# Delta rule into two MoE layers: another order of the first two chunks, group 0 inverted on two engines, fewer weights loaded at the start

## The chip, the cores and the metric

The kernel runs on one core of a Trainium2 chip. Its engines are TensorE (PE, with PEld for its weight loads), VectorE (DVE), ScalarE (ACT), GpSimd (POOL) and SyncE (SP), which issues every transfer. The metric is the time on the device in microseconds (us) of one execution, as a median over runs.

## The reference

Three stages in a row; each feeds the next:

```python
k_n = k / (norm(k) + 1e-6)                       # 4 batches x 8 heads, 768 steps, head size 48
for t in range(S):                               # attention by the delta rule, state D x D per head
    y[t] = q[t] @ state
    state += beta[t] * outer(k_n[t], v[t] - k_n[t] @ state)
x = y as 3072 tokens x 384
h = x @ w_in;  g = h if h >= 1, 0 if h <= -1, else (h + 1)**2 / 4;  x = g @ w_out     # 384 -> 2048 -> 384
h = x @ w_in2; g = relu(h)**2;                                      out = g @ w_out2  # the same sizes
```

## The kernel before

**Tiling.** The 768 steps are cut into 24 chunks of 32 steps; a chunk holds 128 tokens (4 batches). Chunks are gathered twice: in blocks of 2 or 3 (`SIZES`), whose tokens go through the MoE layer together, and in groups of 2 or 4 (`GROUPS`), whose triangular 32 x 32 systems are inverted together. Block 0 is chunks 0 and 1, and so is group 0; group 1 is chunks 2 to 5, group 2 chunks 6 to 9.

**A chunk.** `gram` (L268) multiplies keys with keys and queries on PE and masks the result. `tri` (L334) inverts a group's systems by forward substitution: `step(j)` (L396) is one product and one sum of j x (w-1-j) elements, w the width; a product and a sum depend on each other, so an inverse is a chain of small operations on one engine. All groups share one tile, `tx`, for the inverse; `row2` (L383) writes its start, `end` (L414) transposes the result into `gp`. Group 0 is inverted in two halves of 16 columns, both in one instruction on DVE, and put together by `joined` (L424) with matmuls `ld` and `dld`; `rows` transposes what these need into `d`. The other groups are inverted whole, on POOL. `chunk_steps` (L457) is what follows: `ks`, `tr`, `qs`, `ku`, `pu`, `xt`; the last gives the MoE's input, `xh` and its low part `xl`. `value` (L254) scales a chunk's values on POOL.

**A weight.** Weights come as 64-bit numbers: 32 tiles of 128 x 384 for layer 1 (16 of `w_in`, 16 of `w_out`, in the order in which the MoE asks for them; here x = 0 to 31). A weight's way has four steps: ACT scales it (L164), DVE joins its bits (L172, L175), ACT rounds it to the high part (L186), DVE subtracts that for the low part (L190). PE's hidden tile f (`hidden`, L565) needs both parts of weight x = 2f-1 (for f over 1), the output tile f (`out1`, L603, two hidden tiles later) those of x = 2f+2. Layer 2's weights are read back later and split on POOL and DVE (L237).

**What sets the order.** Up to L725 the kernel stands in one `manual_schedule` for all engines: every engine takes its instructions as the code is written. From L727 only PE's order is the code's. The others' is set by the framework when the kernel is built, by priorities in the code and by when its own model thinks that inputs are ready; each engine then keeps that order strictly. `more_w1` (L674) advances the conversion of layer 1's weights by one step for several weights at a time; before block 0 it runs 12 times, then once in each of the 32 slots of block 0 (two slots for each hidden tile). `put(n, slot, f)` places other work in slots: `end` of group 1 in slot 18, `tri_put` the inverses of groups 2 and on.

**The loads.** `first1(EAGER)` issues the first 18 weights on SP at the start, behind the first keys and queries; each conversion's second step lets `ahead` issue loads up to `AHEAD` = 8 further. Every raw weight has a tile of its own, whose place its two parts take over. Six of the last weights' tiles serve the first chunks before that (`spare`, L313).

Of the kernel before, what the change touches and what calls it, by code (L numbers as in the profile page):

```python
# [25 lines left out]
def kernel(  # L26
# [38 lines left out]
    EAGER = 18  # L65
    AHEAD = 8
# [129 lines left out]
    def weight_items(w):  # L196
# [137 lines left out]
    def tri(n, eng, halves=False):  # L334
# [9 lines left out]
        def two(t, rows, cols):  # L344

            a = t[:, rows, cols]
            (ps_, p_), (rs_, r_), (cs_, c_) = a.ap
            return bass.AP(a.tensor, a.offset, [[ps_, p_], [T2 * (T + 1), 2], [rs_, r_], [cs_, c_]])

# [22 lines left out]

        def row():
            if halves:
                d = two(gm, both, both)
                eng.tensor_mul(
                    d, d, r.rearrange("p (a o i) -> p a o i", a=2, o=1)
                    .to_broadcast([P, 2, T2, T2]))
                return
            for e, rs, cs in whole:  # L380
                e.tensor_mul(gm[:, rs, cs], gm[:, rs, cs], across(r, rs, cs))

        def row2():  # L383
            if halves:
                eng.tensor_mul(
                    two(x, both, both), two(gm, both, both),
                    g.rearrange("p (a i o) -> p a i o", a=2, o=1).to_broadcast([P, 2, T2, T2]))
            else:
                for e, rs, cs in whole:
                    e.tensor_mul(x[:, rs, cs], gm[:, rs, cs], down(g, rs, cs))  # L390
# [516 lines left out]
```

## Time and profile before

| | |
|---|---|
| median of 3 runs | 1054.86 us (1054.44 to 1056.35) |
| the profiled execution's own time | 1054.6 us |
| its span in the profile | 1052.9 us |
| PE busy | 989.3 us (94%), x14440 |
| DVE, ACT, POOL busy | 611.5, 454.3, 313.2 us |
| PE's busy share in the first four 40ths of the span (26.3 us each) | 0.4, 0.3, 0.5, 0.8 |
| the chain that ended last, by engine | PE 81%, DVE 11%, nothing the profile shows ("issue") 4%, ACT 2% |

PE is the engine with the most work, and from the fifth 40th on it is busy 90% or more of nearly every slice. So the time goes where PE waits: 1052.9 less 989.3 us, most of it in the first 140 us. In the rows below an operation is named by engine, line, what it writes and reads, and its size as partitions x elements; "x2" is a count; in brackets stand the engine's idle time before and what ended it. "issue" is a wait for nothing that the profile shows. A row of a stretch gives the busy time of PE, PEld, DVE, ACT and POOL in this order; PEclk is the granted clock of TensorE, 1.00 being the higher of its two levels (2.4 GHz).

### The profile page before, as it was taken

To read this page: it belongs to the slowest core of one execution; us is meant where nothing else is said; L and a number is where in the kernel's file an instruction comes from. 1 tells how busy PE (TensorE), PEld (TensorE's weight loads), DVE (VectorE), ACT (ScalarE), POOL (GpSimd) and SP (SyncE) were. 2 spreads that over 40 slices of the span, in tenths; PEclk is the share of its full clock that TensorE was granted. 3 is DMA by queue.
4 is the path that set the end of the run, shared out by engine and by line. 5 is a ranking of instruction groups with operands and counts; after the bars stand their busy time and mean duration, and the time that the engine had idled before them with its cause. 6 is when DMAs were issued, how large, how long until landed. Compare 5 with 4: busy or idle time off the path is not lost.

```text
span 1052.9 us, 33012 instructions
## 1 busy us (share of the span) xinstructions
PE 989.3 (94%) x14440; PEld 945.0 (90%) x14440; DVE 611.5 (58%) x1125; ACT 454.3 (43%) x931; POOL 313.2 (30%) x456
## 2 busy tenths in 40 slices
PE   4358898999999999999999999999999999999998
PEld 4347788898899998999999999999999999999998
DVE  6879765675575666767545577543434343444333
ACT  2346544445444444545445554433333333333332
POOL 4690681294039208608600123110101010010000
PEclk9997999999999999999999999999999999999999
DMA  9942144352451441512111223010101010000000
GB/s 297 326 121 77 33 124 134 88 150 73 130 152 48 148 134 33 167 56 70 31 42 55 77 90 121 16 45 1 45 1 46 1 45 1 24 1 24 1 23 23
DMA packets 36049, 80.89 MB, mean 77 GB/s; under 512 B 4544, under 2 KB 18368, under 8 KB 35904
## 3 DMA queue, kind: packets, MB, share of 16 engines
q1 hardware_dynamic: 35904, 78.78, 24.8%
q8 instruction: 113, 1.85, 0.8%
q14 instruction: 32, 0.26, 0.1%
HBM read 63.03 MB, written 15.73 MB: 75 GB/s over the span
## 4 chain that ended last, share of the span: by engine, by line
PE 81%; DVE 11%; issue 4%; ACT 2%; DMA 1%; SPq 0%; DVEq 0%; ACTq 0%
PE acc L555 36%; PE h L555 35%; PE tr L486 2%; PE yy L506 2%; PE sps L517 2%; PE yy L472 2%; DVE g L582 1%; DVE g L584 1%; PE g L281 1%; PE ks L472 1%; DVE gl L593 1%; DVE wl L172 1%; DVE wl L175 1%; DVE gp L415 1%; PE xt L540 1%
## 5 line engine op out<-in xcount | busy, mean ns | idle before, releaser
L555 PE MATMUL h<-xh,w 128*128 128x384 f32 (+1 forms) x1632 | 320.4, 332 | 1.8 <-ACT r L581 1.3
L555 PEld LDWEIGHTS h<-xh,w 128*128 128x128 f32 x1632 | 272.7, 190 | 6.8 <-ACT r L581 1.8
L593 DVE TENSOR_TENSOR gl<-g,gh 128x384 fp32r<-128x384 f32 (+1 forms) x272 | 169.5, 623 | 134.3 <-ACT gh L592 128.8
L592 ACT CAST gh<-g 128x384 fp32r<-128x384 f32 (+1 forms) x272 | 135.0, 496 | 209.3 <-DVE g L584 106.0
L555 PE MATMUL h<-xl,w 128*128 128x384 f32 (+1 forms) x816 | 179.8, 329 | 1.3 <-DVE xl L543 1.3
L555 PE MATMUL acc<-gh,w 128*128 128x384 f32 (+1 forms) x864 | 168.5, 331 | 3.8 <-ACT gh L592 3.8
L587 DVE TENSOR_TENSOR g<-r 128x384 f32<-128x384 f32 x128 | 71.4, 558 | 157.4 <-ACT r L586 157.4
L555 PE MATMUL acc<-w,gh 128*128 128x384 f32 x768 | 155.6, 337 | 2.0 <-DVE e L600 2.0
L586 ACT ACTIVATE r<-h,zero 128x384 f32<-128x384 f32 x128 | 74.5, 582 | 166.1 <-PE h L555 166.1
L555 PEld LDWEIGHTS acc<-gh,w 128*128 128x128 f32 x864 | 136.9, 191 | 9.8 <-ACT gh L592 4.2
L555 PEld LDWEIGHTS h<-xl,w 128*128 128x128 f32 x816 | 141.5, 190 | 1.9 <-DVE xl L543 1.9
L555 PEld LDWEIGHTS acc<-w,gh 128*128 128x128 f32 x768 | 136.3, 188 | 2.3 <-ACT gh L592 2.3
L581 ACT ACTIVATE r<-h,one 128x384 f32<-128x384 f32 (+1 forms) x144 | 78.6, 546 | 89.4 <-PE h L555 84.9
L411 POOL TENSOR_TENSOR t<-tx,gm 128x30 f32<-128x30 f32 (+9 forms) x180 | 109.6, 609 | 19.9 <-DVE tx L390 6.4
L412 POOL TENSOR_TENSOR tx<-tx,t 128x30 f32<-128x30 f32 (+9 forms) x180 | 108.4, 602 | 13.7
L584 DVE SCALAR_TENSOR_TENSOR g<-r,g 128x384 f32<-128x384 f32 (+1 forms) x144 | 88.8, 617 | 36.6 <-ACT g L583 34.8
L582 DVE TENSOR_SCALAR g<-r 128x384 f32<-128x384 f32 (+1 forms) x144 | 63.6, 442 | 79.5 <-ACT r L581 78.9
L642 POOL CAST xh<-x2r 128x1152 fp32r<-128x1152 f32 x8 | 9.5, 1186 | 292.9 <-PE h L555 246.1
L583 ACT ACTIVATE g<-g 128x384 f32<-128x384 f32 (+1 forms) x144 | 70.6, 490 | 59.4 <-DVE g L582 58.3
L555 PE MATMUL acc<-gl,w 128*128 128x384 f32 (+1 forms) x432 | 91.5, 320 | 2.6 <-DVE gl L593 2.6
L555 PE MATMUL acc<-w,gl 128*128 128x384 f32 x384 | 88.0, 337 | 0.0
L555 PEld LDWEIGHTS acc<-gl,w 128*128 128x128 f32 x432 | 72.4, 190 | 3.3 <-DVE gl L593 3.3
(94 smaller groups left out, 835.9 us busy)
## 6 DMA issues: line engine op xcount, KB each, us to landing
raw<-in_w_dram SPq DMA_DIRECT2D x64, 384.0 KB, 6.3
kqt<-in_kq_dram SPq DMA_DIRECT2D x88, 192.0 KB, 3.8
kv<-in_kv_dram SPq DMA_DIRECT2D x24, 384.0 KB, 3.1
w2f<-wl SPq DMA_DIRECT2D x32, 192.0 KB, 3.5
w2r<-w2f SPq DMA_DIRECT2D x16, 384.0 KB, 3.0
x2r<-x SPq DMA_DIRECT2D x8, 576.0 KB, 4.4
out_dram<-e SPq DMA_DIRECT2D x24, 192.0 KB, 2.0
x<-e SPq DMA_DIRECT2D x18, 192.0 KB, 2.3
```

The source lines that it names most:

```text
L411: eng.tensor_mul(t, by.to_broadcast(shape), of.to_broadcast(shape))
L412: eng.tensor_add(rest, rest, t)
L472: per_bh(lambda b, h, p, pd: nc.tensor.matmul(o[p, h], kqt[c][pd, b // 2, h, x * T:(x + 1) * T], st[pd, b // 2, h], start=h == 0, stop=x = ...
L555: nc.tensor.matmul(o, *((r, l) if swap else (l, r)), **flags)
L581: marks[0] = nc.scalar.activation(r, h, AF.Relu, bias=one)
L582: marks[1] = nc.vector.tensor_scalar(g, r, 2.0, 0.5, ALU.min, ALU.mult)
L583: nc.scalar.activation(g, g, AF.Square)
L584: nc.vector.scalar_tensor_tensor(g, r, -1.0, g, ALU.add, ALU.max)
L586: marks[0] = nc.scalar.activation(r, h, AF.Relu, bias=zero)
L587: marks[1] = nc.vector.tensor_mul(g, r, r)
L592: nc.scalar.copy(ghi, g)
L593: nc.vector.tensor_sub(glo, g, ghi.bitcast(F32))
```

## The change

1. **Group 0's inverse** runs its two halves as separate instructions, the first on DVE, the second on POOL (`halves=(V, G)`). The masks of the grams around it go from POOL to DVE, behind the inverse.
2. **The first two chunks' chain** stands in the manual part for all engines, link by link; `rows` stands ahead of `end`. The conversions' steps stand behind the chain's links: 6 of them before block 0 instead of 12, in the last half of the chain.
3. **Loads.** Ten weights are loaded at the start instead of 18. The eleventh (x = 10) takes its tile over from `cross`, so its load waits until chunk 1 has read that; loads of later chunks' keys, queries and values are ordered behind it (`quiet`). Weights from x = 17 on go through a ring of three tiles, each loaded three ahead.
4. **The low part** of weights from x = 20 on (12 of 32) is subtracted on POOL instead of DVE.

The core of the diff:

```diff
-    EAGER = 18
-    AHEAD = 8
+    EAGER = 10
+    OWN = 17
+    ALONE = 20
...
     def load_w(x, key):
         w, f, i = key
         pool, tag, bufs = ring, "raw", RAW
-        if w == 0:
+        if w == 0 and x < OWN:
             pool, tag, bufs = wp, f"w{i}{f}", 1
         raw = raws[key] = pool.tile([P, DM, 2], I32, tag=tag, bufs=bufs, name="raw")
-        nc.sync.dma_start(raw.rearrange("p a b -> p (a b)"), (w1, w2)[w][f, i].bitcast(I32))
+        with after[0]():
+            ins = nc.sync.dma_start(
+                raw.rearrange("p a b -> p (a b)"), (w1, w2)[w][f, i].bitcast(I32)
+            )
+        if w == 0 and x == EAGER:
+            after[0] = lambda: tc.issue_after(ins.ins)
...
-            nc.vector.tensor_sub(lo, box["t"], hi.bitcast(F32))
+            (nc.vector if x < ALONE else nc.gpsimd).tensor_sub(lo, box["t"], hi.bitcast(F32))
...
-            r[1] = lambda: (s1(), ahead(x + 1 + (RAW if w else AHEAD)))
+            r[1] = lambda: (s1(), ahead(x + 1 + RAW))
...
         def ahead(end):
+            if w == 0 and turn[0] is not None:
+                end = min(end, EAGER)
...
-    spare = {
-        name: f"w{i}{NF - f}" for name, i, f in
-        (("u0", 1, 1), ("u1", 1, 2), ("cross", 0, 1), ("z", 1, 3), ("l", 0, 2), ("d", 1, 4))
-    }
+    spare = {"cross": f"w1{EAGER // 2 - 1}"}
+    for x, name in enumerate(("u0", "u1", "z", "l", "d", "t")):
+        spare[name] = f"w{x % 2}{NF - 1 - x // 2}"
...
+        parts = whole
+        if halves:
+            parts = [(e, *[slice(T2 * i, T2 * i + T2)] * 2) for i, e in enumerate(halves)]
...
         def step(j):
...
+            ts = []
+            for i, e in enumerate(halves or (eng,)):
+                lo, hi = (T2 * i, T2 * i + T2) if halves else (0, T)
+                w = hi - lo - 1 - j
+                pool, tag = (wp, spare["t"]) if i else (ring, "t0")
+                t = pool.tile([P, j, w], F32, tag=tag, bufs=1, name="t")
+                ts.append((e, lo, hi, t))
+                e.tensor_mul(
+                    t,
+                    x[:, lo:lo + j, lo + j:lo + j + 1].to_broadcast([P, j, w]),
+                    gm[:, lo + j:lo + j + 1, lo + j + 1:hi].to_broadcast([P, j, w]),
+                )
+            for e, lo, hi, t in ts:
+                rest = x[:, lo:lo + j, lo + j + 1:hi]
+                e.tensor_add(rest, rest, t)
...
+    def quiet(load, c):
+        with after[0]():
+            load(c)
...
-        begin, pre, steps, end = tri(0, V, True)
+        begin, pre, steps, end = tri(0, V, (V, G))
...
-        go([gram(c, late=2, eng=G) for c in range(GFIRST[1], GFIRST[2])])
+        masks1 = [gram(c, late=2) for c in range(GFIRST[1], GFIRST[2])]
         cross_gram(0, 1)
-        masks = [gram(c, 1, 2, late=2, eng=G) for c in range(HEADS)]
+        masks = [gram(c, 1, 2, late=2) for c in range(HEADS)]
         go(steps)
         for c in range(HEADS):
             value(c)
-        go(masks)
+
+        rows0()
         end()
-        rows0()
+        for c in range(HEADS):
+            ld0(c)
+        go(masks1)
+        for c in range(HEADS):
+            dld0(c)
+        chains = [chunk_steps(c) for c in range(HEADS)]
+        (k0, t0, q0, p0, _, x0), (k1, t1_, q1, p1, _, x1) = chains
+        go([k0, t0])
         begin, pre, steps, end1 = tri(1, G)
         begin()
-        ins = go(pre[:-2])
-        behind[0] = lambda: tc.issue_after(ins.ins)
+        go(masks)
+        k1()
+        go(pre[:-2])
+        go([q0, p0, t1_])
+        go(pre[-2:])
+        go(steps)
+        more_w1(2)
+        q1()
+        x0()
+        more_w1(2)
+        p1()
+        more_w1(1)
+        x1()
+        more_w1(1)
...
-        for m, fs in enumerate([[k0, t0], [k1], [q0, p0], [t1_], [q1], [x0], [p1], [x1]]):
-            go(fs)
-            if m < 4:
-                more_w1(3)
         behind[0] = lambda ins=marks[2]: tc.issue_after(ins.ins)
         turn[0] = None
-        load_kv(HEADS)
+        first1(EAGER + RAW)
+        quiet(load_kv, HEADS)
```

How instructions stand now, at three places. The lines' numbers are each kernel's own: L411, L412, L172, L175 and L190 of before are L401, L408, L181, L184 and L199 of after.

**DVE, behind group 0's last step.** Before: `gp` is the inverse's transpose, then `d`, then group 1's start and the first conversions (`wl` from `raw`).

```order
L412 TENSOR_TENSOR tx<-tx,t 128x2x14
L415 STREAM_TRANSPOSE gp<-tx 128x32x32
L433 STREAM_TRANSPOSE d<-tx 128x16x32
L351 STREAM_TRANSPOSE gm<-gp 128x32x32
L246 RECIPROCAL st_549<-st_547 128x32
```

After, from the same place on; `kv<-kv,ks` is chunk 1's step `ks`.

```order
L408 TENSOR_TENSOR tx<-tx,t 128x14
L429 STREAM_TRANSPOSE d<-tx 128x16x32
L411 STREAM_TRANSPOSE gp<-tx 128x32x32
L308 TENSOR_TENSOR gp<-gp,mask 128x8x2x32 x4
L446 TENSOR_TENSOR gp<-gp,w 128x8x16 x2
L355 STREAM_TRANSPOSE gm<-gp 128x32x32
L308 TENSOR_TENSOR gp<-gp,mask 128x256 x2
L478 TENSOR_TENSOR kv<-kv,ks 128x384
L257 RECIPROCAL st_746<-st_744 128x32
```

`d` went ahead of `gp`, and four masks, the two joins (L446), two more masks and chunk 1's subtraction came ahead of group 1's start; the conversions stand behind that.

**POOL, in the middle of group 2's inverse** (steps 15 to 18 of 30; step j's elements are j x (31-j)). Before:

```order
L411 TENSOR_TENSOR t<-tx,gm 128x240
L412 TENSOR_TENSOR tx<-tx,t 128x15x16
L411 TENSOR_TENSOR t<-tx,gm 128x240
L412 TENSOR_TENSOR tx<-tx,t 128x16x15
L411 TENSOR_TENSOR t<-tx,gm 128x238
L412 TENSOR_TENSOR tx<-tx,t 128x17x14
L411 TENSOR_TENSOR t<-tx,gm 128x234
L257 TENSOR_TENSOR kv<-kv,nt 128x384
```

After; `w_2105`, `w_2163`, `w_2228` and `w_2286` are the weights x = 28 to 31.

```order
L401 TENSOR_TENSOR t<-tx,gm 128x240
L408 TENSOR_TENSOR tx<-tx,t 128x15x16
L401 TENSOR_TENSOR t<-tx,gm 128x240
L199 TENSOR_TENSOR w_2105<-wl,w_2105 128x384
L408 TENSOR_TENSOR tx<-tx,t 128x16x15
L199 TENSOR_TENSOR w_2163<-wl,w_2163 128x384
L268 TENSOR_TENSOR kv<-kv,nt 128x384
L401 TENSOR_TENSOR t<-tx,gm 128x238
L199 TENSOR_TENSOR w_2228<-wl,w_2228 128x384
L408 TENSOR_TENSOR tx<-tx,t 128x17x14
L199 TENSOR_TENSOR w_2286<-wl,w_2286 128x384
```

The last four low parts stand among steps 16 and 17 of the inverse; five more (x = 23 to 27) stand among its steps 4 to 10, and three (x = 20 to 22) ahead of its first step.

**PE, at the end of block 0**, after: `h` is a hidden tile, `acc` an output tile.

```order
L502 MATMUL yy<-kv,gp 32x48 x32
L551 MATMUL h<-xh,w_2163 128x256 x6
L551 MATMUL h<-xl,w_2163 128x256 x3
L536 MATMUL xt<-ident,kv 128x128 x3
L551 MATMUL acc_1265<-gh,w_2105 128x256 x2
```

PE's order is the same in both kernels; `w_2163` is what hidden tile 15, the last of block 0, multiplies with.

## Rows read from the trace of the kernel before

**Rows 1.** Stretches: start:end, length, busy us (count) per engine, PEclk, DMA share, GB/s.

```profile
15.00:55.00 40.00, 15.78 (x758) 14.52 (x751) 35.96 (x73) 14.13 (x31) 24.64 (x35) 1.00 1.04 340
...
60.00:66.00 6.00, 4.49 (x106) 3.46 (x107) 0.90 (x2) 2.53 (x6) 5.29 (x10) 1.00 0.23 68
...
66.00:102.00 36.00, 26.57 (x461) 23.98 (x464) 35.73 (x78) 23.04 (x54) 14.29 (x23) 0.81 0.27 79
```

**Rows 2.** Chain that ended last: start us, length us, what.

```profile
27.02 2.07 DVE gp L415
...
30.76 2.31 issue
...
49.93 1.50 PE ks L466 x64
...
58.91 1.43 issue
```

**Rows 3.** Timeline (start us, us, engine, line, what, idle before): inverse of group 0.

```profile
15.19 0.18 DVE L411 TENSOR_TENSOR t<-tx,gm 128x28 f32<-128x28 f32 x1
...
19.64 2.52 POOL L297 TENSOR_TENSOR gp<-gp,mask 128x512 f32<-128x512 f32 x2 [6.41 <-ACT gp L294]
...
19.67 1.36 DVE L411 TENSOR_TENSOR t<-tx,gm 128x108 f32<-128x108 f32 x1
```

**Rows 4.** DVE by line, 66.1 to 81 us: count, busy us, mean ns.

```profile
L175 DVE SCALAR_TENSOR_TENSOR wl<-wt,wl 128x384 int32<-128x384 int32 x7 | 5.3, 771 | 0.0
...
L190 DVE TENSOR_TENSOR w<-wl,w 128x384 fp32r<-128x384 f32 x7 | 5.0, 718 | 0.0
...
L172 DVE TENSOR_SCALAR wl<-raw 128x384 int32<-128x384 uint32 x7 | 4.6, 662 | 0.0
```

**Rows 5.** The same, 81 to 102.2 us.

```profile
L175 DVE SCALAR_TENSOR_TENSOR wl<-wt,wl 128x384 int32<-128x384 int32 x12 | 6.7, 557 | 0.0
...
L190 DVE TENSOR_TENSOR w<-wl,w 128x384 fp32r<-128x384 f32 x11 | 6.3, 571 | 0.0
...
L172 DVE TENSOR_SCALAR wl<-raw 128x384 int32<-128x384 uint32 x11 | 3.9, 354 | 0.0
...
L297 DVE TENSOR_TENSOR gp<-g,mask 128x512 f32<-128x512 f32 x3 | 2.1, 684 | 0.0
```

**Rows 6.** Timeline: DVE and POOL around the first conversions.

```profile
32.21 0.35 DVE L246 RECIPROCAL st<-st 128x32 f32<-128x32 f32 x1 [0.42 <-ACT st L245]
...
34.61 2.12 DVE L172 TENSOR_SCALAR wl<-raw 128x384 int32<-128x384 uint32 x4
...
37.41 0.48 POOL L411 TENSOR_TENSOR t<-tx,gm 128x30 f32<-128x30 f32 x1 [1.43 <-DVE tx L390]
...
41.89 0.29 DVE L450 TENSOR_TENSOR gp<-gp,w 128x128 f32<-128x128 f32 x1 [2.42 <-PE w L445]
```

**Rows 7.** Timeline: DVE, POOL and PE, hidden tiles 5 to 15 of block 0.

```profile
101.82 0.42 DVE L593 TENSOR_TENSOR gl<-g,gh 128x256 fp32r<-128x256 f32 x1
...
110.24 2.13 DVE L415 STREAM_TRANSPOSE gp<-tx 128x1024 f32<-128x1024 f32 x1
...
117.16 0.22 DVE L391 COPY tx<-st 128x32 f32<-128x32 f32 x1
...
119.27 0.24 POOL L412 TENSOR_TENSOR tx<-tx,t 128x30 f32<-128x30 f32 x1
...
138.41 0.80 POOL L412 TENSOR_TENSOR tx<-tx,t 128x240 f32<-128x240 f32 x1
...
116.08 1.65 PE L555 MATMUL acc<-gh,w 128*128 128x256 f32 x6
...
135.41 0.98 PE L555 MATMUL h<-xh,w 128*128 128x256 f32 x6
```

**Rows 8.** POOL by line and shape, whole span: count, busy us, mean ns.

```profile
L237 POOL TENSOR_TENSOR w<-w2r,w 128x384 fp32r<-128x384 f32 x16 | 16.6, 1039 | 60.1 <-ACT w L231 57.6 <-PE acc L555 2.5
```

**Rows 9.** The page's DMA issues: tile, queue, op, count, KB each, us to landing.

```profile
raw<-in_w_dram SPq DMA_DIRECT2D x64, 384.0 KB, 6.3
```

More of the change, by code (lines that the diff above doesn't have):

```diff
@@ L115 @@
     kqt, kvt, gp, nt, xh, xl = {}, {}, {}, {}, {}, {}
+    marks = [None] * 3
     def load_kq(c):
@@ L148 @@
     raws = {}
+    after = [nullcontext]
     def load_w(x, key):
@@ L205, in item @@
             if w == 0:
-                r = part_stages(keys[x], box)
+                r = part_stages(x, keys[x], box)
             else:
@@ L288, in gram @@
             kqg.pop(c)
-            if late < 2:
+            if turn[0] is None:
                 load_kg(c + KG)
@@ L332, with tri @@
     T2 = T // 2
-    def tri(n, eng, halves=False):
+    def tri(n, eng, halves=()):
         x = tx
@@ L342, in flat @@
             return t.rearrange("p j i -> p (j i)")[:, diag]
[L344 to L348, printed above, removed]
         def begin():
@@ L371, in gamma2 @@
             return nc.vector.tensor_mul(g, g, bet[:, n, :])
+        parts = whole
+        if halves:
+            parts = [(e, *[slice(T2 * i, T2 * i + T2)] * 2) for i, e in enumerate(halves)]
         def row():
[L374 to L380, printed above, removed]
+            for e, rs, cs in parts:
                 e.tensor_mul(gm[:, rs, cs], gm[:, rs, cs], across(r, rs, cs))
         def row2():
[L384 to L390, printed above, removed]
+            for e, rs, cs in parts:
+                e.tensor_mul(x[:, rs, cs], gm[:, rs, cs], down(g, rs, cs))
             nc.vector.tensor_copy(flat(x), g)
@@ L396, in step @@
         def step(j):
-            if halves:
-                w = T2 - 1 - j
-                t = ring.tile([P, 2, j, w], F32, tag="t0", bufs=1, name="t")
-                rest = two(x, slice(0, j), slice(j + 1, T2))
-                by = two(x, slice(0, j), slice(j, j + 1))
-                of = two(gm, slice(j, j + 1), slice(j + 1, T2))
-                shape = [P, 2, j, w]
-            else:
-                w = T - 1 - j
-                t = ring.tile([P, j, w], F32, tag="t0", bufs=1, name="t")
-                rest = x[:, 0:j, j + 1:T]
-                by = x[:, 0:j, j:j + 1]
-                of = gm[:, j:j + 1, j + 1:T]
-                shape = [P, j, w]
-            eng.tensor_mul(t, by.to_broadcast(shape), of.to_broadcast(shape))
-            eng.tensor_add(rest, rest, t)
+            ts = []
[13 more added lines that the diff above has]
+                e.tensor_add(rest, rest, t)
         def end():
@@ L718 @@
             value(c)
-        go(masks)
+        rows0()
         end()
-        rows0()
+        for c in range(HEADS):
[6 more added lines that the diff above has]
+        go([k0, t0])
         begin, pre, steps, end1 = tri(1, G)
         begin()
-        ins = go(pre[:-2])
-        behind[0] = lambda: tc.issue_after(ins.ins)
+        go(masks)
[12 more added lines that the diff above has]
+        more_w1(1)
     ENGINES = {mybir.EngineType.PE}
     with tc.manual_schedule(engines=ENGINES):
-        for f in (ld0, dld0):
-            for c in range(HEADS):
-                f(c)
-        go(pre[-2:])
-        go(steps)
-        chains = [chunk_steps(c) for c in range(HEADS)]
-        (k0, t0, q0, p0, _, x0), (k1, t1_, q1, p1, _, x1) = chains
-        for m, fs in enumerate([[k0, t0], [k1], [q0, p0], [t1_], [q1], [x0], [p1], [x1]]):
-            go(fs)
-            if m < 4:
-                more_w1(3)
         behind[0] = lambda ins=marks[2]: tc.issue_after(ins.ins)
         turn[0] = None
-        load_kv(HEADS)
+        first1(EAGER + RAW)
+        quiet(load_kv, HEADS)
         for c in range(KG):
-            load_kg(KQ + KG + c)
+            quiet(load_kg, KQ + KG + c)
         SL = 2 * NF
```

6 lines of the change are left out of this document (2 added, 4 removed).

## The prediction

> **What bounds the kernel now.** The page's slices say that PE is busy 90% or more from about 130 us on, so the change, which touches only the first two chunks and the 32 weights of layer 1, can win or lose only before that. I read three things there, in this order.
>
> First the chain of waits up to 66 us [rows 2]. It leaves DVE with the inverse's transpose at 27.0 us and runs through PE's small matmuls; `ks`, 64 of them, takes 1.50 us. Between those PE stops five times for "issue", from 2.31 us at 30.8 to 1.43 us at 58.9, together 19.0 us. No instruction and no transfer of the program ends these stops. They fall where the transfers are saturated (DMA share 1.04, 340 GB/s from 15 to 55 us); from 60 to 66, with a share of 0.23, there is none [rows 1]. I read them as PE's own code waiting behind the weights.
>
> Second the stretch from 66 to 102 us [rows 1]: DVE is busy 35.7 of 36 us, PE 26.6 at a mean clock of 0.81. Block 0 has begun, but DVE is the bound. It converts weights, and until about 81 us at a worse price than later: the three DVE steps of one take 0.771 + 0.718 + 0.662 = 2.15 us [rows 4] beside POOL's inverse of group 1, and 0.557 + 0.571 + 0.354 = 1.48 us after it [rows 5].
>
> Third the end of block 0 [rows 7]: from about 102 us PE is the bound, and it reaches hidden tile 15 at 135.4 us. POOL meanwhile inverts group 2 and nobody waits for it. That is what the change alters most.
>
> **The front, part by part.** *Inverse of group 0.* Now one instruction of 28 elements costs DVE 0.18 us [rows 3]; the change gives DVE 28 of half the size and POOL as many. A POOL operation of 30 elements takes 0.24 us [rows 7], with the gap to the next about 0.32, so 28 take 9.0 us, with a little for sizes up to 56 about 10. If the engines hold each other up in every pair, DVE's 28 x 0.2 = 5.6 come on top: 15.7. From a start at 15.5 us (one product more on POOL ahead of it) this ends between 25.5 and 31.2 us; I take 27.5, nearer to the low end, because such small operations hold little. The old inverse ended at 27.0. So the split in itself wins nothing; what POOL's masks cost the old one (1.36 us for an operation beside a POOL mask [rows 3]) goes into it.
>
> The row first: at 19.67 us a DVE product that otherwise takes under 0.3 us took 1.36, until the POOL mask begun at 19.64, of 1.26 us apiece, was done [rows 3]. The Trainium skill says why: "SBUF — State Buffer", section "Who interferes with whom", has VectorE and GpSimd share a pair of SBUF ports by an exclusive lock, which a VectorE operation with two SBUF inputs needs. By that rule alone the two halves would go one after the other; the trace agrees for large operations, and no row shows two small ones side by side. This is the second rival.
>
> *The chain.* From 27.5: the transpose 2.07 [rows 2], four masks that are now on DVE ahead of the join, at 0.684 each for this size [rows 5], 2.7; the join 0.29 [rows 6]; `tr` and `ks` at 1.50 each [rows 2]; an evacuation and a subtraction at about 0.57 [rows 5], 1.1. That is 36.7 us for chunk 1's subtraction. `d` is transposed beside POOL's half, and `ld` with it, so they cost nothing; were that cover gone, 1.0 and 2 us. Group 1's start then takes what it took from 32.21 to 37.41 less the four conversion steps in between, 2.12 [rows 6]: 3.1 us. With 0.7 for stops that remain the conversions begin at 40.5 us, where they began at 34.6 [rows 6]: 5.9 later. The stops themselves go because ten weights are 3.9 MB, 11.6 us at 340 GB/s, so the transfers are done some 27 us into the span.
>
> *What DVE has to do by the end of hidden tile 5's work, at 102.2 us* (101.82 + 0.42 [rows 7]). In the old order 27 low parts stand ahead of that and 30 of the two steps before; in the new 20 and 23. Seven conversions fewer, at 1.48 less the overlap of neighbours, about 1.25: 8.7 us won. DVE's idle time is filled: 2.4 us [rows 6] and 6.0 - 0.9 = 5.1 us [rows 1], 7.5 us won at most, nothing at least. The later start loses 5.9. POOL's inverse of group 1 now runs beside busy DVE where 7.5 us of it were beside an idle one: 7.5 x (1 - 1.48/2.15) = 2.3 lost. Together **8.0 us earlier**; bounds 3 (idle mostly not filled, start a little late) and 9.4, since PE has no more than 36 - 26.6 = 9.4 us to give [rows 1].
>
> *Loads.* x = 10 waits on SP for chunk 1's `qs`, and the loads of x = 11 and 12, values, keys and queries are queued behind it; ten conversions lie between, over 20 us at 2.15, so I cost it at nothing. From x = 20 on a load waits for the conversion three ahead of it: 3 x 1.25 = 3.8 us against 6.3 to landing [rows 9], at worst 2.5 us in each of four turns, 10 us on ACT and DVE. There PE is the bound, and the same weights are late on POOL anyway, so this is not added.
>
> **The end of block 0.** The low parts of x = 23 to 29 stand in POOL's queue among the first 16 steps of group 2's inverse, and POOL keeps its order. That inverse can't begin before `end` of group 1, since `tx` is shared. Before, `end` starts at 110.24, the diagonal's copy is done at 117.38, POOL's step 1 at 119.51 and step 16 at 139.21 [rows 7]: nothing needed it. Now DVE's queue from `end` to that copy holds 2.13 + two times 0.354 + 0.684 + two of about 0.57 + two times 0.557 + 0.22 = 6.0 us; add the same 2.1 to the end of step 1; 19.7 to the end of step 16, as before; and seven low parts at 1.04 [rows 8], 7.3. So x = 29 is ready 35.1 us after `end` starts. Hidden tile 15, which needs it, came 135.41 - 110.24 = 25.2 us after: it will be **9.9 us late**, tile 14 a part of that (x = 27). Bounds: 4.5, if POOL does a low part in DVE's 0.571 and step 1 needn't wait; 13.9, if each also waits for one DVE operation. DVE gets 12 x 0.571 us back, but it isn't the bound there. Chunk 6, the next that needs group 2, comes much later.
>
> Behind a wait PE is slow at first: six matmuls took 1.65 us behind its wait for chunk 2, and 0.98 in the stream [rows 7]; two such sets, **1.3 us** (0.7 to 2).
>
> **Sum.** - 8.0 + 9.9 + 1.3 = + 3.2 us. Span 1052.9 to 1056.1, own time 1054.6 to 1057.8; the median lies 0.26 above the profiled run: **1058.1 us**. From the bounds the case goes from - 4.2 (9.4 won, 4.5 and 0.7 lost) to + 12.9 (3 won, 13.9 and 2 lost).
>
> **Rivals.** *The low parts are in time (faster).* If POOL reached x = 29 within 25.2 us of `end`, only the front counts: 1054.9 - 8.0 = 1046.9 us. It decides where 30 operations and 7 low parts take 25.2 - 8.1 = 17.1 us, 0.46 each; the 30 took 0.66 [rows 7]. For it: POOL is otherwise idle there, and the inverse could start earlier than I think. Against it: the order puts 16 steps ahead, and the steps' times are measured.
>
> *The two halves go one after the other.* The inverse ends at 31.2 instead of 27.5, all later work on DVE 3.7 us later: 1058.1 + 3.7 = 1061.8 us. It is the rule above as a mechanism of this kernel; the large operations speak for it, the small size of these against.
>
> *The stops stay.* If half of the 19.0 us remain though the weights are fewer, the front loses instead: 1058.1 + 9.5 = 1067.6 us. Rows 1 speak against it.
>
> **How the numbers follow.** Forecast 0.55, low parts in time 0.22, halves serial 0.17, stops stay 0.06. Within 0.2%, some 2.1 us, about what a measurement of this kernel can tell from no change: 0.17 of the forecast's 0.55, 0.02 and 0.01 of the next two, 0.20. Faster: 0.05 of the forecast and 0.20 of the first rival, 0.25. Slower: 0.33 + 0.16 + 0.06 = 0.55. The range leaves out the lower half of the first rival and the top of the last: 1047 to 1067 us.
>
> **What would show it.** In the changed kernel's trace: PE's stops before block 0 a few us in all instead of 19; POOL's half done at 25 to 31 us; the first hidden tile some 15 us earlier than now; tile 5's work done near 94 us; then PE waiting at tiles 14 and 15 for POOL's L199, some 10 us together. No such wait on POOL would prove me wrong, and so would DVE still being late at tile 5.

## The result and the profile after

The changed kernel takes 1066.49 us (median of 4 runs, 1064.07 to 1068.01) against 1054.93 us of the kernel before on the same chip: ratio 1.0105, 95% interval 1.0082 to 1.0128, so 11.6 us slower. The direction was forecast, and the time is inside the range, 0.5 us below its upper end; the loss forecast was 3.2 us. The profiled execution took 1068.0 us, its span 1066.3.

The page's busy times of PE, DVE and POOL after, and its chain by engine:

```profile
PE 994.7 (93%) x14440; PEld 949.4 (89%) x14440; DVE 616.6 (58%) x1119; ACT 452.9 (42%) x931; POOL 330.8 (31%) x492
...
PE 81%; DVE 8%; issue 4%; DMA 3%; POOL 3%; ACT 1%; SPq 1%; DVEq 0%; ACTq 0%; POOLq 0%
```

PE has the same 14440 matmuls. Of the 13.4 us by which this span is longer, 5.4 are matmuls that took longer (994.7 instead of 989.3 us, at a mean granted clock of 0.976 instead of 0.990) and 8.0 are waits. POOL, 3%, is new on the chain, and DMA has 3% instead of 1%. The stretches of [rows 1] after (start:end, length, busy us of PE, PEld, DVE, ACT, POOL, granted clock, DMA share, GB/s):

```profile
15.00:55.00 40.00, 24.16 (x1011) 22.01 (x1007) 28.35 (x67) 12.00 (x27) 18.69 (x47) 0.89 0.46 158
60.00:66.00 6.00, 1.10 (x64) 0.94 (x64) 6.00 (x9) 2.55 (x6) 5.45 (x8) 0.77 1.04 306
66.00:102.00 36.00, 21.77 (x338) 19.02 (x338) 34.25 (x60) 18.99 (x43) 27.55 (x37) 0.71 0.46 133
```

PE does 24.2 us of work in the first stretch instead of 15.8, so the chain did get ahead. From 66 to 102 us DVE is nearly as full as before, but POOL is busy 27.6 us beside it instead of 14.3, and PE does 21.8 us instead of 26.6. Where the lead goes shows in the start of block 0's hidden tiles (us, from PE's timeline; counted as in the prediction, tile 16 is block 1's first):

| hidden tile | before | after | difference |
|---|---|---|---|
| 0 | 65.68 | 52.31 | -13.4 |
| 3 | 82.83 | 73.62 | -9.2 |
| 5 | 93.09 | 90.97 | -2.1 |
| 7 | 102.55 | 101.99 | -0.6 |
| 8 | 104.78 | 108.43 | +3.6 |
| 12 | 123.05 | 126.65 | +3.6 |
| 14 | 131.23 | 142.80 | +11.6 |
| 16 | 137.93 | 151.03 | +13.1 |

After tile 16 the two run alike. So there are two losses: 12.8 us between tiles 0 and 7, nearly all of it ahead of tile 5, where DVE never rests, and 13.7 us from there to tile 16.

### The profile page after: what moved, and what is told of

Same layout as the page of the kernel before. It is cut to its first block, busy times and chain, and to the rows that moved or that the text cites. A ratio compares the mean times of both kernels' runs of the same rounds, so it can differ in the third digit from the quotient of the medians.

```text
span 1066.3 us, 33065 instructions
## 1 busy us (share of the span) xinstructions
PE 994.7 (93%) x14440; PEld 949.4 (89%) x14440; DVE 616.6 (58%) x1119; ACT 452.9 (42%) x931; POOL 330.8 (31%) x492
## 3 DMA queue, kind: packets, MB, share of 16 engines
q1 hardware_dynamic: 35904, 78.78, 24.5%
## 4 chain that ended last, share of the span: by engine, by line
PE 81%; DVE 8%; issue 4%; DMA 3%; POOL 3%; ACT 1%; SPq 1%; DVEq 0%; ACTq 0%; POOLq 0%
PE acc L551 35%; PE h L551 35%; PE g L292 2%; PE tr L482 2%; PE yy L502 2%; DMA raw<-in_w_dram 1%; PE yy L468 1%; PE sps L513 1%; DVE g L579 1%; PE ks L468 1%; DVE g L577 1%; DMA kqt<-in_kq_dram 1%; DVE gl L588 1%; POOL tx L408 1%; POOL t L401 1%
## 5 line engine op out<-in xcount | busy, mean ns | idle before, releaser
L551 PE MATMUL h<-xh,w 128*128 128x384 f32 (+1 forms) x1632 | 323.7, 335 | 7.1 <-ACT r L576 4.9
L551 PEld LDWEIGHTS h<-xh,w 128*128 128x128 f32 x1632 | 275.7, 192 | 12.5 <-ACT r L576 5.9
L408 POOL TENSOR_TENSOR tx<-tx,t 128x84 f32<-128x84 f32 (+18 forms) x194 | 114.3, 589 | 14.4
L401 POOL TENSOR_TENSOR t<-tx,gm 128x84 f32<-128x84 f32 (+18 forms) x194 | 111.8, 576 | 18.2 <-DVE tx L387 4.0
L579 DVE SCALAR_TENSOR_TENSOR g<-r,g 128x384 f32<-128x384 f32 (+1 forms) x144 | 92.1, 640 | 38.2 <-ACT g L578 36.4
L577 DVE TENSOR_SCALAR g<-r 128x384 f32<-128x384 f32 (+1 forms) x144 | 63.0, 438 | 79.0 <-ACT r L576 78.1
```

The source lines that it names most:

```text
L401: e.tensor_mul(t, x[:, lo:lo + j, lo + j:lo + j + 1].to_broadcast([P, j, w]), gm[:, lo + j:lo + j + 1, lo + j + 1:hi].to_broadcast([P, j, w]),
L408: e.tensor_add(rest, rest, t)
L551: nc.tensor.matmul(o, *((r, l) if swap else (l, r)), **flags)
L577: marks[1] = nc.vector.tensor_scalar(g, r, 2.0, 0.5, ALU.min, ALU.mult)
L579: nc.vector.scalar_tensor_tensor(g, r, -1.0, g, ALU.add, ALU.max)
```

## The experiments

The theories: **C**, DVE pays for every instruction that runs beside POOL's inverse of group 1; **L**, the later weights' loads hold ACT; **P**, POOL's low parts are late (the prediction's); **S**, PE's stops for "issue" set the chain; **F** and **O**, the conversions start too late, or stand in the wrong order. The comparisons' kernel before took 1053.8, 1054.6 and 1054.1 us (medians) beside the first, second and third group of runs, so a difference of two kernels' medians can differ by some 1 us from that of their ratios. A tile's start comes from one profiled execution: tile 0 started at 52.31 us in the changed kernel and at 53.95 in the first run below, whose instructions up to there are the same, so a difference of 1.6 us or less between two profiles shows nothing by itself.

### The end of block 0: low parts and loads

`e1_low_dve`: `- ALONE = 20`, `+ ALONE = 99`.

> The changed kernel, with all low parts left on DVE (none on POOL). Theory P (POOL's late low parts hold the conversions' buffers and hidden tiles 13 to 15): DVE's 2.67 us stop for POOL at 131.7 us, PE's 2.80 us for the subtraction behind it and the 1.26 us of tile 15 go, block 1's first hidden tile starts 5 to 9 us earlier than 151.0, and the whole takes 1058 to 1061 us against 1066.5. Theory L (the later weights' loads, three ahead, hold ACT): its 5.8 us of stops for loads stay, DVE gets 12 more subtractions of 0.56 us, and the time is 1064 to 1070 us.

1066.2 us, ratio 1.0112 (1.0082 to 1.0141): the same as the changed kernel. Tile 16 starts at 152.4. PE's wait for POOL is gone, but its waits for DVE's subtraction (3.4 us) and ACT's copy (3.0 us) stay. Theory P falls.

`e2_deep_loads`:

```
-    OWN = 17
+    OWN = 99
-            r[1] = lambda: (s1(), ahead(x + 1 + RAW))
+            r[1] = lambda: (s1(), ahead(x + 1 + (RAW if w else 8)))
-        first1(EAGER + RAW)
+        first1(EAGER + 8)
```

> The changed kernel, with the weights from the 18th on loaded into their own places too and eight ahead instead of three. Theory L: ACT's 5.8 us of stops for loads (94 to 129 us) go, tile 13 starts some 4 us earlier, and the whole takes 1060 to 1063 us. Theory P: ACT's stops go too, but POOL's low parts are as late as before, so block 1 starts within 1.5 us of 151.0 and the time is 1065 to 1068 us.

1059.8 us, ratio 1.0052 (1.0037 to 1.0067): 6.7 us faster than the changed kernel (5.6 by the two ratios). ACT waits for no load any more, tile 16 starts at 144.45 instead of 151.03. What it cured, in ACT's timeline of the changed kernel (start, us, instruction, and in brackets the idle time before it and what ended it):

```profile
100.28 0.57 ACT L173 ACTIVATE wt<-raw 128x384 f32<-128x384 f32 x1 [2.19 <-DMA raw<-in_w_dram]
...
128.12 0.55 ACT L173 ACTIVATE wt<-raw 128x384 f32<-128x384 f32 x1 [1.96 <-DMA raw<-in_w_dram]
```

Six such waits make 5.8 us. The time is theory L's, but the gain is not where these waits stand: tile 13 comes 1.4 us earlier, not 4. Behind the second wait, ACT comes late to the copy L506 that PE's `xt` waits for (2.62 us at 130.56). With the deep loads PE waits for it as long, since ACT then waits for DVE:

```profile
129.00 0.90 PE L536 MATMUL xt<-ident,kv 128*128 128x128 f32 x3 [2.69 <-ACT kv L506]
```

4.3 of the 6.6 us at tile 16 are won between tiles 7 and 10. There ACT's row has another order. In the changed kernel the `r` that tile 8 waits for (3.99 us) stands behind group 2's norms, L256, and these wait for DVE; with the deep loads it stands ahead of them:

```profile
107.67 0.35 ACT L256 ACTIVATE st<-gm,tiny 128x32 f32<-128x32 f32 x1 [3.22 <-DVE gm L355]
107.93 0.45 ACT L576 ACTIVATE r<-h,one 128x256 f32<-128x256 f32 x1
```
```profile
103.89 0.47 ACT L576 ACTIVATE r<-h,one 128x256 f32<-128x256 f32 x1
...
107.37 0.35 ACT L256 ACTIVATE st<-gm,tiny 128x32 f32<-128x32 f32 x1 [3.01 <-DVE gm L355]
```

So the ring of three costs its 6.7 us, but through ACT's waits or through the order that the framework makes with it: no run tells these apart.

`e3_both`: both edits.

> Both of these at once. If loads and POOL's low parts hold the second half of block 0 together and add up, block 1 starts at 138 to 143 us and the time is 1053 to 1058 us, what the front alone gives. If neither is the cause (the front is: conversions that begin at 46.3 us and run beside POOL's inverse), block 1 stays later than 147 us and the time above 1062 us.

1060.4 us, ratio 1.0062 (1.0046 to 1.0078), no better than the deep loads alone; 10 runs spread from 1056.9 to 1063.8, and the profiled one, span 1055.1, lies at the low end, with tile 16 at 142.3. The low parts add nothing, so some 6 us of the change's loss must have other causes.

### The front: what DVE pays beside POOL

`e6_no_inverse1`: `- go(steps)`, `+ go(steps[:1])` for group 1. `e11_before_no_inverse1`: the same in the kernel before.

> The changed kernel, which leaves out 29 of the 30 steps of group 1's inverse on POOL (so its output is another), to measure what DVE pays beside them. Theory C (contention): beside those steps a conversion's three DVE instructions take 2.6 us (0.93, 0.77 and 0.87 at 62 to 72 us), alone 1.4 (0.55, 0.34 and 0.54 at 92 to 102 us), so the 38.7 us from hidden tile 0 (52.3) to hidden tile 5 (91.0), in which DVE never rests, shrink to 26 to 29 us, tile 5 starts at 78 to 82 us, and the whole takes 1053 to 1059 us. Theory O (the order in DVE's row holds the tiles' own work back, whatever the price of one instruction): tile 5 starts after 85 us and less than 5 us is won.

> The kernel before, which leaves out 29 of the 30 steps of group 1's inverse on POOL (so its output is another), against the same cut in the changed kernel, where tile 5 came 18.5 us earlier. Theory C (the change pays more for POOL's steps than the kernel before did): here tile 5 comes only 4 to 8 us earlier than 93.1, at 85 to 89 us, and the whole takes 1046 to 1050 us, so that the change's loss to contention is 10 to 14 us. Rival: tile 5 comes 15 us or more earlier here too, and the time is below 1042 us; then contention is no difference between the two.

One execution each: 1046.8 us, 20 less than the changed kernel, and 1049.7 us, 4 less than the kernel before. That without the steps the changed kernel is 2.9 us the faster isn't shown: single executions of the kernel before go from 1051.5 to 1057.8 us. Tile 5 starts at 72.46 instead of 90.97 in the one (18.5 us earlier) and at 88.05 instead of 93.09 in the other (5.0). The stretch from tile 0 to tile 5 of the four kernels, in this order: after, the same without the steps, before, the same without the steps (columns as in the stretches above):

```profile
52.30:91.00 38.70, 20.46 (x329) 18.52 (x330) 38.70 (x56) 18.76 (x42) 35.33 (x50) 0.68 0.58 154
```
```profile
51.20:72.50 21.30, 17.63 (x329) 15.85 (x329) 21.30 (x56) 18.20 (x42) 12.39 (x2) 0.91 1.03 281
```
```profile
65.70:93.10 27.40, 18.74 (x329) 17.08 (x329) 27.40 (x56) 17.10 (x39) 14.52 (x24) 0.81 0.29 89
```
```profile
66.60:88.00 21.40, 16.84 (x328) 15.07 (x328) 21.40 (x56) 16.85 (x39) 5.02 (x2) 1.00 0.38 113
```

In all four DVE does 56 instructions without a pause (the same kinds; in the first, one conversion step stands in for a mask). They take 21.3 and 21.4 us alone, whatever the DMA share (1.03 and 0.38), and 38.7 and 27.4 us beside POOL's 50 and 24. So the steps cost 17.4 us after and 6.0 before, and the difference, 11.4 us, is the first loss. Without the steps the lead at tile 0, 15.4 us (51.17 against 66.59), is still there at tile 5, 15.6 us. DVE by line in that stretch, after and without the steps (count, busy us, mean ns):

```profile
L184 DVE SCALAR_TENSOR_TENSOR wl<-wt,wl 128x384 int32<-128x384 int32 x14 | 12.6, 908 | 0.1
L199 DVE TENSOR_TENSOR w<-wl,w 128x384 fp32r<-128x384 f32 x14 | 11.3, 810 | 0.0
L181 DVE TENSOR_SCALAR wl<-raw 128x384 int32<-128x384 uint32 x15 | 10.2, 688 | 0.0
```
```profile
L199 DVE TENSOR_TENSOR w<-wl,w 128x384 fp32r<-128x384 f32 x14 | 7.7, 551 | 0.0
L184 DVE SCALAR_TENSOR_TENSOR wl<-wt,wl 128x384 int32<-128x384 int32 x13 | 7.1, 551 | 0.0
L181 DVE TENSOR_SCALAR wl<-raw 128x384 int32<-128x384 uint32 x15 | 5.3, 357 | 0.0
```

One conversion costs 0.908 + 0.810 + 0.688 = 2.41 us beside POOL and 1.46 without. The kernel before ran much of POOL's inverse while PE's chain stood still for "issue". DVE's conversions were dear there too (two of their three instructions took 0.9 to 1.0 us from 48 to 56 us), but held nothing up: without the steps tile 0 came no earlier. The change moved the inverse under the stretch that DVE bounds. Theory C holds for the first loss.

It doesn't for the second. From tile 5 to tile 16 the changed kernel takes 60.1 us with the steps and 60.1 without, the kernel before 44.8 and 45.1. One thing that differs there is how many conversions are left. DVE's second step of them in that stretch, before (93.1 to 137.9 us) and after (91 to 151 us):

```profile
L175 DVE SCALAR_TENSOR_TENSOR wl<-wt,wl 128x384 int32<-128x384 int32 x8 | 4.4, 563 | 0.0
```
```profile
L184 DVE SCALAR_TENSOR_TENSOR wl<-wt,wl 128x384 int32<-128x384 int32 x15 | 11.1, 759 | 0.0
```

Fifteen instead of eight, and each dearer: those from 121 us on stand beside POOL's inverse of group 2. In `e5_early` below it is 11, and the stretch takes 51.8 us.

`e7_inverse1_first`:

```
         end()
+        go(masks1)
+        begin, pre, steps, end1 = tri(1, G)
+        begin()
+        go(pre)
+        go(steps)
...
-        go(masks1)
...
-        begin, pre, steps, end1 = tri(1, G)
-        begin()
...
-        go(pre[:-2])
...
-        go(pre[-2:])
-        go(steps)
```

> The changed kernel, with group 1's inverse begun right behind its masks (28.9 us), ahead of group 0's correction, in DVE's idle 6.3 us, instead of behind chunk 0's links. Theory C: POOL's steps begin at 35 to 37 us instead of 46.0 and end at 81 to 84 instead of 92.2, so that some 10 us of DVE's work ahead of tile 5 run alone instead of beside them: tile 5 starts 3 to 5 us earlier than 91.0, and the whole takes 1060 to 1064 us against 1066.5. Theory O: the chain's links wait for the inverse's first instructions on DVE and ACT, hidden tile 0 starts 2 us or more later than 52.3, and the time is 1065 to 1069 us.

1061.2 us, ratio 1.0059 (1.0045 to 1.0072), 5.3 us faster than the changed kernel, though tile 0 starts 1.7 us later (54.02). POOL's steps run from 35.6 to 76.2 us, tile 5 starts at 85.71, 5.3 us earlier. The time and the start are theory C's, the end is earlier than it said; 1.7 us at tile 0 is too little to tell whether O has a part.

`e5_early`:

```
         end()
+        more_w1(4)
...
         go(masks1)
+        more_w1(1)
...
         go(masks)
+        more_w1(1)
...
         x0()
-        more_w1(2)
-        p1()
         more_w1(1)
+        p1()
         x1()
```

> The changed kernel, with conversion steps already behind group 0's inverse (four), behind each of the two sets of masks (one each), two behind group 1's first steps and two beside the last links: ten before the first hidden tile's end instead of six, in DVE's idle 6.3 us before 35.2 and 2.7 us before 41.5. Theory F (front: what costs is the conversions' start at 46.3 us): four conversions of some 1.9 us less afterwards, tile 5 starts 6 to 8 us earlier than 90.97, and the whole is 5 to 8 us faster, 1058 to 1061 us. If loads and POOL decide the second half anyway (L or P), tile 5 is as much earlier but the whole gains under 3 us: 1064 to 1066 us. If the steps get in the way of the chain's links, the first hidden tile slips by 2 us or more from 52.3 and the gain is below 4 us at tile 5.

1057.1 us, ratio 1.0025 (1.0009 to 1.0041): 9.4 us faster, more than F said, but not where it said. Tile 5 comes only 2.0 us earlier (89.00); the 10 us come from tile 8 on (tile 16 at 140.82). Low parts done at tiles 0 and 5: 2 and 16 after, 6 and 20 here. DVE does 14 between them in both; what is done ahead is saved behind tile 5. Of the 10 us, 5.9 lie between tiles 7 and 10: here too ACT's row has tile 7's `r` ahead of L256.

`e8_early_deep`: `e5_early` and `e2_deep_loads`.

> e5_early and e2_deep_loads together. If the two gains are of different stretches (conversions ahead of tile 5; loads from 94 us on), they add: block 1 starts at 134 to 137 us and the whole takes 1049 to 1053 us. If the early conversions already took the load stops' place (both gains lie in tiles 12 to 15), block 1 starts at 139 to 142 us and the time is 1055 to 1058 us.

1055.2 us, ratio 1.0004 (0.9988 to 1.0019): 11.3 us of the 16.1 that a plain sum gives. Tile 16 starts at 140.1, as the second case has it, but the overlap isn't in tiles 12 to 15. The time between starts of tiles (us):

| tiles | after | deep loads | early | both |
|---|---|---|---|---|
| 7 to 10 | 14.4 | 10.1 | 8.5 | 9.3 |
| 10 to 16 | 34.7 | 32.9 | 29.5 | 27.7 |

Behind tile 10 the gains add (1.8 and 5.1 against 7.0). Between tiles 7 and 10 both remove the same stop of tile 8.

`e9_all`: `e7_inverse1_first`, the deep loads, and:

```
             dld0(c)
+        more_w1(2)
...
         go([k0, t0])
+        more_w1(2)
...
         k1()
+        more_w1(1)
...
         x0()
-        more_w1(2)
+        more_w1(1)
```

> e7_inverse1_first with the deep loads and ten conversion steps before the first hidden tile's end, spread behind the correction and the links. If contention, loads and the late start of the conversions are the three costs, POOL is done by 84 us, block 1 starts at 131 to 135 us and the whole takes 1044 to 1051 us, below the kernel before. If the conversions then run beside POOL all the same and delay the links, hidden tile 0 starts after 54.5 us and the time stays above 1053 us.

1051.6 us, ratio 0.9968 (0.9952 to 0.9985): **faster than both kernels**, by 14.9 and 3.0 us. Tile 16 starts at 136.1, POOL's steps end at 78.1. The stretch from 26 to 46 us, after and here:

```profile
26.00:46.00 20.00, 11.52 (x673) 10.71 (x673) 9.82 (x20) 3.84 (x10) 2.16 (x2) 1.00 0.02 6
```
```profile
26.00:46.00 20.00, 11.93 (x634) 11.04 (x637) 16.50 (x33) 6.19 (x16) 11.43 (x21) 1.00 0.02 6
```

DVE works 16.5 us there instead of 9.8 and POOL 11.4 instead of 2.2, while PE does the same. It falls just short of the expected 1044 to 1051; tile 0 slips to 54.7, which is the rival's mark, but the rival's time, above 1053, does not come.

`e12_two_halves_pool`, against `e9_all` (`l` and `z` of `joined` are for up to four chunks, two places each):

```
-        begin, pre, steps, end1 = tri(1, G)
+        begin, pre, steps, end1 = tri(1, G, (G, G))
...
+        save1, rows1, ld1, dld1 = joined(1)
...
-        put(0, HEAD - 1, *later(end1))
+        put(0, 6, *later(rows1))
+        put(0, 7, *later(end1))
+        for c in range(GROUPS[1]):
+            put_a(0, 11 + c, lambda c=c: ld1(c))
+            put_a(0, 14 + c, lambda c=c: dld1(c))
```

> e9_all, with group 1's inverse in two halves on POOL and joined on PE afterwards as group 0's is: 56 small instructions on POOL instead of 60 large ones, and for it 256 small matmuls, eight copies on ACT and some 7 us on DVE (a transposition of 1.05 us, subtractions and two more memsets on POOL). Theory C: POOL's steps end before 62 us instead of 81, DVE's work from there on runs alone, tile 5 starts at 79 to 83 us (86.5 in e9_all) and the whole takes 1044 to 1049 us. Rival: the joining's stops on PE (256 matmuls, some two stops of 1.7 us) and its 7 us on DVE eat what is won: tile 5 after 85 us, 1050 to 1055 us.

1066.4 us, ratio 1.0108 (1.0084 to 1.0132). C's part came true: POOL's steps end at 58.3 us, tile 5 starts at 77.6. But neither theory saw what follows. PE then waits, in its timeline:

```profile
63.84 0.39 PE L292 MATMUL g<-kqt 48*32 48x64 f32 x2 [4.74 <-DMA kqt<-in_kq_dram]
...
84.88 0.39 PE L292 MATMUL g<-kqt 48*32 48x64 f32 x2 [5.59 <-DMA kqt<-in_kq_dram]
...
124.99 1.50 PE L485 MATMUL tr<-kv,gp 32*32 32x48 f32 x64 [9.57 <-DVE kv L481]
```

That the late `kqt` loads stand behind weights which wait on SP for the joining's borrowed places is my reading, and wasn't tried apart.

### The first part alone, and the loads at the start

`e4_before_halves`, against the kernel before, with the changed kernel's `row`, `row2` and `step`:

```
-        begin, pre, steps, end = tri(0, V, True)
+        begin, pre, steps, end = tri(0, V, (V, G))
-        go([gram(c, late=2, eng=G) for c in range(GFIRST[1], GFIRST[2])])
+        masks1 = [gram(c, late=2) for c in range(GFIRST[1], GFIRST[2])]
-        masks = [gram(c, 1, 2, late=2, eng=G) for c in range(HEADS)]
+        masks = [gram(c, 1, 2, late=2) for c in range(HEADS)]
...
+        rows0()
+        end()
+        go(masks1)
         go(masks)
-        end()
-        rows0()
```

> The kernel before, with the first part of the change alone: group 0's inverse in halves on DVE and POOL, and the masks behind it moved from POOL to DVE. Theory S (PE's stops set the chain in the kernel before, so an earlier inverse only waits longer at the next of them): the inverse's halves end near 24 us as in the changed kernel, the stops behind it grow by what is won, hidden tile 0 starts within 1 us of 65.7 and the time stays within 2 us of 1054. Rival: the 2.5 us won in the inverse reach hidden tile 0 (63 us) and the end, 1051 to 1052 us.

1055.55 us, ratio 1.0015 (1.0001 to 1.0029): no gain. POOL's half ends by 24.5 us, the stop behind it is 3.99 us instead of 2.31 [rows 2], and tile 0 starts at 67.7, 2.1 us later; 1.9 of these it is behind already ahead of the inverse (PE's second set starts at 16.45 instead of 14.56). So the mark at tile 0, within 1 us, is missed as it stands and met without that late start. Theory S holds for the time: PE's wait for `d`, 1.66 us before, is gone, and the next stop is 1.68 us longer.

`e10_loads18`: `- EAGER = 10`, `+ EAGER = 18` (and `OWN = 18`).

> The changed kernel, with eighteen weights loaded at once as before instead of ten. Theory S: PE's six stops between 27 and 46 us (10.6 us) grow to 20 us or more, hidden tile 0 starts at 60 to 65 us instead of 52.3. If DVE's work beside POOL's inverse then moves along with it (theory C), tile 5 starts at 97 to 103 us and the whole takes 1070 to 1078 us. Rival: the start of the chain doesn't count, since DVE is the limit: tile 5 within 3 us of 91 and the time 1064 to 1069 us.

1075.2 us, ratio 1.0196 (1.0176 to 1.0216): 8.7 us slower than with ten, and tile 5 starts at 98.14, both as theory C has it. Tile 0 starts at 59.85, and the six stops make 17.4 us, a little short of S's marks. PE's longest stops of this kernel behind 27 us, and those of the changed one:

```profile
33.27 1.52 PE L433 MATMUL z<-d,l 32*32 32x16 f32 x98 [4.00 <-issue]
39.62 1.51 PE L441 MATMUL w<-gp,z 32*32 32x16 f32 x97 [4.45 <-issue]
45.70 1.01 PE L482 MATMUL tr<-kv,gp 32*32 32x48 f32 x35 [3.94 <-issue]
```
```profile
30.81 1.51 PE L433 MATMUL z<-d,l 32*32 32x16 f32 x98 [1.53 <-issue]
34.41 1.51 PE L441 MATMUL w<-gp,z 32*32 32x16 f32 x97 [1.70 <-issue]
38.29 1.00 PE L482 MATMUL tr<-kv,gp 32*32 32x48 f32 x35 [1.74 <-issue]
45.51 0.61 PE L462 MATMUL yy<-u,cross 32*32 32x48 f32 x36 [1.75 <-issue]
```

So the loads lengthen a stop from 1.7 to 4 us, as the prediction read it; the rest stays without any load.

## Why the prediction was right and wrong

**The inverse's halves: too dear, and right in effect by luck.** POOL's half ends at 24.2 us, forecast 27.5 with bounds from 25.5. DVE and POOL side by side, with 54 and 56 elements:

```profile
18.35 0.33 DVE L401 TENSOR_TENSOR t<-tx,gm 128x56 f32<-128x56 f32 x1
18.71 0.33 DVE L408 TENSOR_TENSOR tx<-tx,t 128x56 f32<-128x56 f32 x1
```
```profile
18.32 0.29 POOL L408 TENSOR_TENSOR tx<-tx,t 128x54 f32<-128x54 f32 x1
18.68 0.29 POOL L401 TENSOR_TENSOR t<-tx,gm 128x56 f32<-128x56 f32 x1
```

Each engine starts one every 0.36 us, and the end at 24.2 us is far from the 31.2 of the rival in which the halves go one after the other: it falls. DVE does pay, 0.33 us for 50 to 56 elements, where the kernel before took 0.21 for 52 (at 15.63 us). That the split alone wins nothing came true, but not for the reason given: the new inverse was to end no earlier than the old, at 27.0 us; it ended 2.8 us earlier, and PE's stops took that (`e4_before_halves`).

**The chain's stops: mis-sized, 0.7 forecast, 6.7 measured** (1.53 + 1.70 + 1.74 + 1.75). Three of them, 4.97 us, stand ahead of chunk 1's subtraction, which ends at 42.0 (41.49 + 0.55) instead of 36.7 us; group 1's start then takes 4.3 us instead of 3.1, and the conversions begin at 46.3 instead of 40.5. As the inverse ended 3.3 us ahead of the forecast, another 3.7 us were lost on the way. That is the step by which `ld` would be covered by POOL's half and cost nothing. PE reaches it only at 28.67 us, behind the second set of grams and their stop of 2.95 us, and DVE stands until `dld` is through:

```profile
27.20 1.54 PE L292 MATMUL g<-kqt 48*32 48x32 f32 x97 [2.95 <-issue]
28.67 0.61 PE L433 MATMUL z<-d,l 32*32 32x16 f32 x30
...
35.16 0.29 DVE L446 TENSOR_TENSOR gp<-gp,w 128x128 f32<-128x128 f32 x1 [6.29 <-PE w L441]
```

The evidence for the stops lay in [rows 2]: 1.43 us at 58.91. The prediction looked for stops from 60 us on; in the stop's own stretch of the kernel before the DMA share (second number from the end) is already 0.07:

```profile
58.90:60.30 1.40, 0.01 (x2) 0.00 (x0) 0.77 (x1) 1.40 (x4) 1.24 (x3) 1.00 0.07 29
```

So a stop of about 1.5 us belongs to PE's code itself. It comes after 128 of these matmuls; between the third and the fourth stop there are 255, and the place in the middle shows none. What is moved meanwhile, in the changed kernel from 28 to 47 us (queue: packets, MB, share), and in a quarter of a microsecond ahead of the first stop and in the stop:

```profile
q8 instruction: 6, 0.10, 2.2%
```
```profile
28.00:28.25 0.25, 0.25 (x37) 0.25 (x31) 0.25 (x2) 0.25 (x1) 0.00 (x0) 1.00 0.27 66
29.25:30.75 1.50, 0.03 (x3) 0.00 (x0) 0.00 (x0) 0.00 (x0) 0.00 (x0) 1.00 0.00 0
```

That is six packets of instructions, some 16 KB each, at 28.2, 31.8, 35.5, 39.4, 42.8 and 46.8 us. The first four come 1.0 to 1.1 us after PE goes on from a stop, and PE goes on from the next stop 2.6 to 2.8 us after a packet; behind that of 39.4 this time had about passed when PE came to the place without a stop. So I read the stops as waits for code; no run changes the code alone. The Trainium skill, "Runtime: NRT & Kernel Launch", section "Instruction fetch mechanics", says that code comes in blocks of 256 instructions, which agrees with 128 matmuls and 128 weight loads, and that this is mostly hidden, which these four stops do not show. The rival in which half of the stops stay was the nearest to this, 9.5 us where 6.7 came.

**DVE's work by the end of tile 5's: the count right, the price and the idle time wrong.** Low parts ahead of that point are 20 instead of 27, as forecast. But it is reached at 103.6 us (103.20 + 0.43) instead of 102.2: 1.4 us later, not 8.0 earlier. From 27 us to that point, before and after:

```profile
27.00:102.24 75.24, 43.36 (x1222) 38.65 (x1226) 66.50 (x127) 37.88 (x87) 43.25 (x67) 0.91 0.58 174
```
```profile
27.00:103.63 76.63, 45.60 (x1248) 40.65 (x1249) 63.85 (x113) 34.03 (x78) 48.01 (x67) 0.78 0.49 141
```

DVE's work falls by 2.7 us, where 6.4 were forecast (8.7 for seven conversions, less 2.3 for contention). Its idle time, 8.7 us before, is 12.8: 4.0 more, where the sum had 1.6 less (7.5 filled, the most that was possible, less 5.9 for the later start). The idle time wasn't filled but moved ahead of the conversions, to the waits of 6.29 us at 35.16 and 2.67 at 41.49. These two, 3.7 and 5.6 us, are the whole error of this term.

The price failed since it was taken from [rows 4], 2.15 us, in a stretch that ends with POOL's last, short steps, and only DVE's formerly idle time was counted as newly contended. From tile 0 to tile 5 a conversion cost 2.41 us and POOL was busy nearly all of the time, 35.3 of 38.7 us instead of 14.5 of 27.4. The cost which [rows 3] had shown for one instruction, 1.36 us beside a POOL mask, was read as a matter of group 0 alone. The Trainium skill, "SBUF — State Buffer", section "Who interferes with whom", calls the ports that the two engines share an exclusive lock. That DVE's time rises by 82% over this stretch agrees with such a lock. That each waits for the whole of the other's instruction isn't shown: the shortest times of the same POOL steps between 130 and 450 us, in the two kernels, add up to some 25 us (an estimate, for 47 of the 50), and with DVE's 21.3 us alone that is more than the 38.7 us.

**Loads costed at nothing: wrong.** 5.8 us of ACT's waits, 6.7 us of the time in `e2_deep_loads`. The prediction bounded them at 10 us and then left them out, because "there PE is the bound, and the same weights are late on POOL anyway". PE is not the bound there: from tile 5 to tile 16 it is busy 45.2 of 60.0 us, where it was 40.5 of 44.8. By the same step the prediction took the conversions that are put off behind tile 5 to cost nothing.

**POOL's low parts: size right, place wrong.** x = 29 is done at 148.6 us, 33.2 us after `end` starts at 115.4; forecast 35.1. But PE waits for it only once:

```profile
148.63 0.86 PE L551 MATMUL h<-xh,w 128*128 128x256 f32 x5 [1.26 <-POOL w L199]
```

The step that failed held tile 15 to its old 25.2 us behind `end`; by then it was 31.6 us behind (146.99), held up by other things, and taking the low parts off POOL won nothing. The term of 9.9 us was not there.

**Slow matmuls, 1.3 us.** Tile 8 found its `r` 3.99 us late: on ACT it stood behind group 2's norms, which waited 3.22 us for DVE's transposition. In the kernel before, the norms (105.90) stand behind that `r` (103.98) in ACT's row, and PE doesn't stop there. Six matmuls then took 1.65 us as in [rows 7], and 1.48 for tile 9, at a granted clock of 0.60 from 106 to 114 us. This stop is new, and no part of the forecast held it. Over the whole span the slower matmuls are 5.4 us, not 1.3.

**The sum.** To tile 5's work -8.0 became +1.4; +11.2 for the rest became +11.7, with put-off conversions, loads and the stop of tile 8 in POOL's place. The shape was right (the lead is won, 13.4 us at tile 0 against some 15 forecast, and more than given back by the end of block 0), the two largest terms were not: the first had the wrong sign, the second wasn't there. That the time falls inside the range is luck. By the prediction's own signs it is wrong: DVE was still late at tile 5, and of some 10 us that PE should wait for POOL there were 1.3.

**Still open**: how the second loss divides between the conversions put off behind tile 5, the loads, and the order of ACT's row at tile 8. Each of `e2_deep_loads` and `e5_early` takes a part of it away, but both change that order too. And what is left between the changed kernel with deep loads (1059.8 us) and the kernel before is not added up: the costs overlap.

## What to carry to other kernels

When a change moves one engine's long work under another's busy stretch, count the instructions that newly run side by side and price them from the stretch where both are busy with the same shapes; a run that leaves that work out, in both kernels, measures it directly. Time won ahead of a full engine is lost there unless that engine's work moves into the gap too, as `e9_all` does. Work that is put off behind a full stretch isn't free because another engine is the bound there now; count it where it lands. And an instruction of the critical chain that stands in its engine's row behind another's wait waits with it, as tile 8's `r` does behind the norms; a change that only moves loads can change that order, so compare the rows before giving a gain to the loads.

## What was unexpected of the hardware

- PE stops 1.5 to 1.75 us after 128 small matmuls although next to nothing but instructions is moved (share 0.02 from 30 to 46 us), and 4 us under load. From a packet of instructions to PE's going on it takes 2.6 to 2.8 us.
- DVE's instruction with one tensor input (L181) is hit as hard as those with two: 357 to 688 ns, against 551 to 908 and 551 to 810.
- Full transfers slow DVE not at all: 551, 551 and 357 ns at a DMA share of 1.03, and 562, 551 and 356 at 0.38 (`e6_no_inverse1`, `e11_before_no_inverse1`).
